# Keys times query into PSUM: the scores of a one-token attention kernel, 16 keys at a time

## The chip, the cores and the metric

The kernel runs on one core of a Trainium2 chip. Such a core has TensorE (PE, matrix products into PSUM), VectorE (DVE), ScalarE (ACT), GpSimd (POOL) and SyncE (SP), which here issues nearly all transfers from the chip's main memory. Each engine has its own list of instructions and waits for others by semaphores. SBUF is the core's working memory of 128 partitions; PSUM is a smaller one of eight banks, each of 512 float32 values per partition. The metric is the time of one execution on the device in microseconds.

## The reference

One decoding step with batch `B` = 2: layer norm, an attention with 32 heads of 128 over a cache of 8192 keys and values per head, and a gate from a small two-layer network.

```python
xn = layernorm(x)                                    # x: 2 x 1 x 512
q = (xn @ wq) as 2 x 32 heads x 1 x 128
scores = einsum("bhqd,bhkd->bhqk", q, k_cache) * 128 ** -0.5     # 8192 keys
p = softmax(scores)
o = einsum("bhqk,bhkd->bhqd", p, v_cache)
s = o as 2 x 1 x 4096 @ wo
g = silu(gelu(layernorm(xn) @ w1 + b1) @ w2 + b2)
out = x + s * g
```

All is float32. K and V are 268 MB each and are read once; that is most of the 559 MB that the kernel reads.

## The kernel before

**Tiling.** The 64 combinations of batch and head are taken two at a time: 32 "pairs" (`N`), numbered 0 to 31. In a pair each of the two heads has 64 partitions, and each partition holds 128 (`KP`) keys of 128 values: a K or V tile of 128 x 16384 float32, 8.4 MB. SBUF has three such buffers: `big0` and `big1` (`KBUF[0]`, `KBUF[1]`) take the K of even and odd pairs, `big2` (`VB`) takes V. Before the pairs begin, a setup computes the query and spreads it so that `Q[:, n, :]` holds in each partition the query of that partition's head, and computes the gate `z`; its weights and intermediate values use the same three buffers and PSUM banks.

**The scores of a pair** are VectorE's work, `scores` (L328). It waits for the K tile, multiplies it by the query and writes the product over K itself (one `tensor_tensor` over 128 x 16384, L332, the query repeated for every key), waits for that, and sums each key's 128 products into `SC` (one `tensor_reduce`, L335). It waits again and takes the maximum over the partition's keys, `MX` (L337). TensorE transposes `MX` into `pm`, VectorE takes from it the negated maximum of each head, `nm` (L339), TensorE spreads that over the partitions (`pn`), and ScalarE computes the exponentials into `PZ` and their sums into `RS` (L351 on). The waits are instructions of their own, made by `take` (L45), which waits for a semaphore and counts it down; by the profile such a wait is one on the engine's own sequencer, "DVEq L45".

**Weighting.** TensorE multiplies `PZ` with V in 32 products (`weighted`, L475); ScalarE copies the sum to `o4`, TensorE folds that into `pt`, and ScalarE keeps it in `OT`. In the time in which TensorE would wait, `unread` (L459) lets it compute products into bank 6 that nobody reads.

**Loops and queues.** VectorE's loop (L342) runs over pairs 0 to 29, two to a turn; the last two pairs stand behind it, the last with K in two halves. ScalarE, TensorE and SP have loops of their own over the same pairs. SP's list (L305 to L325) sets the order of the transfers, all in one queue: K of pair n + 2 when the softmax of pair n has begun (`p_k`, sent by TensorE behind `nm`), then V of pair n + 1 when the weighting of pair n has let go of its buffer (`p_free`). V of the last pair goes to K's buffer, and behind it comes `wo` in eight pieces, into V's buffer.

**The end.** From the kept sums VectorE computes `ZL`, `Z` and `on` (the attention's output, L370 to L377), TensorE multiplies `on` with `wo` as its pieces arrive, 28 columns into `pw` and the rest into `acc` (L526 on), and two VectorE instructions apply the gate and add x.

A single helper line, L51, issues every operation, so the profile's groups are told apart by tile names: `big` is K or V (or the weights that share their place), `sc` the scores.

Of the kernel before, what the change touches and what calls it, by code (L numbers as in the profile page):

```python
# [5 lines left out]
ALU = mybir.AluOpType  # L6
AX = mybir.AxisListType
# [6 lines left out]
class Program:  # L14
# [24 lines left out]
    def wait(self, eng, *tokens):  # L39
        for name, v in self.need(eng, tokens):  # L40
            self.engines[eng].wait_ge(self.sem(name), v)

    def take(self, eng, name, v=1):

        self.engines[eng].wait_ge(self.sem(name), v).then_inc(self.sem(name), -v)  # L45

    def op(self, eng, method, *args, waits=(), sig=None, by=1, quiet=False, **kwargs):
        need = self.need(eng, waits)
        for name, v in need[:-1]:
            self.engines[eng].wait_ge(self.sem(name), v)  # L50
        ins = getattr(self.engines[eng], method)(*args, **kwargs)  # L51
        for name, v in need[-1:]:
            ins._wait_ge(self.sem(name), v)
        if quiet:
            return None
        name = sig or "own_" + eng
        by = 16 if method == "dma_start" else by
        ins.then_inc(self.sem(name), by)
        self.counts[name] += by
        return name, self.counts[name]  # L60


def decode_kernel(nc, x, kc, vc, wq, wo, w1, b1, w2, b2, out):
    P = 128
    B, H, S, DH = kc.shape
# [3 lines left out]
    U = 2  # L69
    HP = P // U  # L70
    KP = S // HP
    HH = H // U
    N = B * HH
# [22 lines left out]
    op, wait, take = pr.op, pr.wait, pr.take  # L96

    def sb(shape, name):
        return nc.alloc_sbuf_tensor(name, list(shape), F32).ap()

    def ps(shape, name):
        return nc.alloc_psum_tensor(name, list(shape), F32).ap()
# [6 lines left out]
    KBUF, VB = rows[:2], rows[2]  # L109
# [24 lines left out]
    Q = sb([P, N, DH], "Q")  # L134
    ident = sb([P, P], "ident")
# [13 lines left out]
    z = sb([P, P], "z")  # L149
# [6 lines left out]
    SC = [sb([P, KP], f"sc{i}") for i in range(2)]  # L156
# [10 lines left out]
    on = sb([P, MB, OC], "on")  # L167
    mod_b = sb([P, R], "mod_b")

    bank = [ps([P, 512], f"bank{i}") for i in range(8)]  # L170
    po = bank[0]
    pm = bank[1]
    pn = bank[2]
    pt = bank[3]
    acc = bank[4][:, :P]
    OA = bank[5][:, :B * (OC + 1)].rearrange("p (b c) -> p b c", c=OC + 1)
# [9 lines left out]
    QH = len(PB) // 2  # L186
# [6 lines left out]
    def pe_n(name, n):  # L193
        return name, n + 1

    t = {}
# [30 lines left out]
    for k in (7, 6, 1, 2, 4, 0):  # L227
# [13 lines left out]
                  op=ALU.add)  # L241
    t["sel"] = op("DVE", "tensor_copy",
                  sel[:, HP:].rearrange("p (b j r) -> p b j r", b=B, r=HG)[:, :, :QT, 0], by_row[:, :B, :],
                  waits=[t["sel0"]])
# [23 lines left out]
    c = op("DVE", "tensor_mul", gu, gh, gh, waits=[a])  # L268
    c = op("DVE", "tensor_scalar", gu, gu, GELU_A, 1.0, op0=ALU.mult, op1=ALU.add, waits=[c])
    c = op("DVE", "tensor_mul", gu, gu, gh, waits=[c])  # L270
    c = op("ACT", "activation", gu, gu, AF.Tanh, scale=GELU_C, waits=[c])
    c = op("DVE", "scalar_tensor_tensor", gu, gu, 1.0, gh, op0=ALU.add, op1=ALU.mult, waits=[c])
# [8 lines left out]
    for part, n0, n1 in (("first", 0, NPB), ("rest", NPB, N)):  # L281
        shape = [BH, n1 - n0, DH]
        t[f"QN {part}"] = op("DVE", "tensor_tensor", out=QN[:, n0:n1, :], in0=q_all.unsqueeze(1).to_broadcast(shape),
                           in1=mine[:, n0:n1].unsqueeze(2).to_broadcast(shape), op=ALU.mult,
                           waits=[t["qall"], t["mine"]])
# [13 lines left out]
    for b in range(B):  # L299
        t["x4"] = op("SP", "dma_start", x4[HB * b::R, :], x[b, 0].rearrange("(j n) -> j n", n=P), sig="d_x4",  # L300
                     waits=[t["x4m"]])
# [26 lines left out]
    def scores(u, q, sems, cuts):  # L328
        k = KBUF[u]
        for name, (c0, c1) in zip(sems, zip(cuts, cuts[1:])):  # L330
            take("DVE", name, 16)
            op("DVE", "tensor_tensor", out=k[:, c0:c1], in0=k[:, c0:c1],  # L332
               in1=q.unsqueeze(1).to_broadcast([P, c1 - c0, DH]), op=ALU.mult, sig="v_t")
            take("DVE", "v_t")
            op("DVE", "tensor_reduce", out=SC[u][:, c0:c1], in_=k[:, c0:c1], axis=AX.X, op=ALU.add, sig="v_r")  # L335
        take("DVE", "v_r", len(sems))
        op("DVE", "tensor_reduce", out=MX, in_=SC[u], axis=AX.X, op=ALU.max, sig="v_mx")  # L337
        take("DVE", "p_m")
        op("DVE", "tensor_reduce", out=nm, in_=pm[:1, :P].rearrange("o (s r) -> o s r", s=U), axis=AX.X,  # L339
           op=ALU.max, negate=True, sig="v_nm")  # L340

    with nc.vector.Fori(0, N // U - 1) as i:  # L342
        take("DVE", "s_q")
        for u in range(U):
            scores(u, Q.rearrange("p (i u) d -> p i u d", u=U)[:, i, u, :], [f"d_k{u}"], (0, KP))
    take("DVE", "s_q")
    scores(0, Q[:, N - U, :], ["d_k0"], (0, KP))
    scores(1, Q[:, N - 1, :], ["d_k1", "d_kl"], HALVES)


    with nc.scalar.Fori(0, N // U) as i:  # L351
        for u in range(U):
# [4 lines left out]
            for s in range(U):  # L357
# [10 lines left out]
                   waits=[t["th"], t["pool"]])  # L368
    shape = [P, N, U * PH]
    t["ZL"] = op("DVE", "tensor_tensor", out=ZL, in0=half.unsqueeze(1).to_broadcast(shape),  # L370
                 in1=RS.unsqueeze(2).to_broadcast(shape), op=ALU.mult, waits=[pe_n("p_z", 0), t["half"]])
# [3 lines left out]
                in1=OT.unsqueeze(2).to_broadcast(shape), op=ALU.mult, waits=[t["OT"], t["blk"]])  # L375
    t["on"] = op("DVE", "tensor_tensor", out=on[:, ::HB, :], in0=OA[:, :, :OC], in1=rl.unsqueeze(2).to_broadcast([P, B, OC]),
                 op=ALU.mult, waits=[t["rl"], t["on0"], pe_n("p_oa", 0)])  # L377
    t["wide"] = op("ACT", "copy", o4, pw, waits=[pe_n("p_w", 0)])
    a = op("DVE", "scalar_tensor_tensor", res, acc, 0.5, gate, op0=ALU.mult, op1=ALU.mult,
           waits=[pe_n("p_acc", 0), t["gate"]])  # L380
    t["res"] = op("DVE", "tensor_add", res, res, x4, waits=[a, t["x4"]])
    t["out"] = op("SP", "dma_start", out.rearrange("b s (j n) -> j (b s) n", n=P), res[::HB, :], sig="d_out",
                  waits=[t["res"]])
# [6 lines left out]
    def mm(dst, w, v, start=True, stop=True, sig=None, waits=(), skip=False):  # L390
        kw = {"skip_group_check": True} if skip else {}
        if sig in PE_EVENTS:
            done.append(sig)
            sig = "pe_setup"
        return op("PE", "matmul", dst, w, v, start=start, stop=stop, waits=waits, sig=sig, quiet=sig is None, **kw)
# [15 lines left out]
    for c in range(ND):  # L411
# [4 lines left out]
        j, k = NF % QT, NF // QT  # L416
# [6 lines left out]
    j, k = NF % QT, NF // QT  # L423
    mm(ph[R * j:R * j + B, k * P:k * P + FT], ones[:1, :B], b1_sb[:, NF * P:], start=False, stop=True, sig="ph")
    by_tile = ident.rearrange("p (j r) -> p j r", r=R)
    for k in range(NH):
        n = min(QT, NF + 1 - k * QT)
        mm(phT[:, k * QT * B:(k * QT + n) * B].rearrange("p (j b) -> p j b", b=B), h_nat[:, k * P:(k + 1) * P],
           by_tile[:, :n, :B], waits=[t["h"]], sig="phT" if k == NH - 1 else None)
    for n in range(NG // QT):  # L430
        for c in range(ND):
            for j in range(QT):
                g = n * QT + j
# [3 lines left out]
    for n in range(NG // QT):  # L437
        for hh in range(HG):
# [3 lines left out]
               waits=[t["sel"], t["qnat"]], sig="pqa" if last else None)  # L442

    for g in range(N // NPB):
        mm(PB[g % len(PB)], sides, QN[:, g * NPB:(g + 1) * NPB, :].rearrange("h n d -> h (n d)"),
           waits=[t["side"], t["QN rest" if g else "QN first"]] + ([t[f"Q{QH}"]] if g >= len(PB) else []),
           sig=f"pb{g}")
    for f in range(NF + 1):
        j = f % QT
        k = P if f < NF else FT  # L450
        mm(pg[R * j:R * j + B, :], hT[:k, f, :], w2_sb[:k, f, :], start=f < QT, stop=f + QT > NF and j != QT - 1,
           waits=[t["hT"], t["w2"], t["mem6"]])
    mm(pg[R * (QT - 1):R * (QT - 1) + B, :], ones[:1, :B], b2_sb, start=False, stop=True, waits=[t["b2"]], sig="pg")
    for j in range(QT):
        mm(pgate[R * j:R * j + MB, :], mod_b[:, :MB], g_nat[:, j * P:(j + 1) * P], waits=[t["g"], t["mod_b"]],
           sig="pgate" if j == QT - 1 else None)
    assert done == PE_EVENTS, done

    def unread(*heads):  # L459

        for n in heads:
            mm(bank[6][:, :n * DH], ident, Q[:, :n, :].rearrange("p n d -> p (n d)"), waits=[t["g"], t[f"Q{QH}"]])

    def softmax(first=False):
        if not first:
            unread(4, 4)
        take("PE", "v_mx")
        op("PE", "transpose", pm[:1, :P], MX, ident, sig="p_m")
        if not first:
            unread(1)  # L470
        take("PE", "v_nm")
        for s in range(U):
            mm(pn[HP * s:HP * (s + 1), :1], srow, nm[:, s:s + 1], sig="p_n" if s == U - 1 else "p_k")

    def weighted(v, last=False):  # L475
        if last:
            unread(4, 2)
        take("PE", "s_pz")
        if not last:
            take("PE", "d_v", 16)  # L480
        for i in range(NT):
            if last and i * JW == HALVES[1]:
                unread(2)
            if last and i * JW in HALVES:
                nc.tensor.wait_ge(pr.sem(f"d_v31{HALVES.index(i * JW)}"), 16)
            j = i % QT
            mm(po[R * j:R * j + U * JW, :], PZ[:, i].rearrange("p s j -> p (s j)"),
               v[:, i * JW:(i + 1) * JW, :].rearrange("p j d -> p (j d)"), start=i < QT, stop=i + QT >= NT,
               sig="p_v" if i == NT - 1 else "p_z" if last and i == 0 else None)
        if last:  # L490
            for b in range(B):
                m = slice(b * HH, (b + 1) * HH)
                mm(OA[:, b, OC:], ZL[:, m].rearrange("p n r -> p (n r)"), ones[:, :1], waits=[t["ZL"]],
                   sig="p_den" if b == B - 1 else None)
            unread(1)
        take("PE", "s_o4")
        for i in range(JW):
            mm(pt[:, :U], o4[:, i * DH:(i + 1) * DH], mod[:, i:U * JW:JW], start=i == 0, stop=i == JW - 1,
               sig="p_t" if i == JW - 1 else "p_free" if i == 0 else None)
# [21 lines left out]
    for b in range(B):  # L521
        h = slice(b * H, (b + 1) * H)
        mm(OA[:, b, :OC], Z[:, h].rearrange("p h r -> p (h r)"), mod, waits=[t["Z"]],
           sig="p_oa" if b == B - 1 else None)
    unread(1)
    for i, (c0, c1) in enumerate(zip(WO_CUTS, WO_CUTS[1:])):  # L526
        for c in range(c0, c1):
            after = [t["on"], t["mem"], (f"d_wo{i}", 16)]
            if c < WIDE:
                j = c % QT  # L530
                mm(pw[R * j:R * j + MB, :], on[:, :, c], wo_sb[:, c, :], start=c < QT, stop=c + QT >= WIDE,
                   waits=after, sig="p_w" if c == WIDE - 1 else None)
# [7 lines left out]
        if c1 == OC - 2:  # L540
            for j in range(QT):
                mm(acc[R * j:R * j + MB, :], mod[:, :MB], o4[:, j * P:(j + 1) * P], start=False, stop=False,
                   waits=[t["wide"]])
# [26 lines left out]
```

## Time and profile before

| | |
|---|---|
| median of the runs | 1300.54 us (2 runs, 1299.89 to 1301.18) |
| the profiled execution | 1299.61 us, span of its profile 1298.3 us |
| VectorE busy | 1135.7 us, 87% of the span, 171 instructions |
| TensorE busy | 460.9 us, 35% |
| ScalarE busy | 72.0 us, 6% |
| DMA | 559.39 MB, mean 431 GB/s, 99.7% of the 16 engines' time in SP's queue |

In the profile's rows the engine is followed by the line, the operation, what it writes and reads, shapes as partitions x elements, and a count. A group's row gives busy time and the mean of one in ns, then the idle time ahead of its instructions and what ended it. In the timeline a row begins with its start and its length in us. TensorE takes a float32 product in two passes, so each product is two rows there. The table of stretches gives for each engine its busy time and, as (x..), its instructions, in the order PE, PEld (weight loads), VectorE, ScalarE, GpSimd; then the TensorE clock granted, the mean busy share of the DMA engines and what they moved.

### The profile page before, as it was taken

To read this page: it belongs to the slowest core of one execution; us is meant where nothing else is said; L and a number is where in the kernel's file an instruction comes from. 1 tells how busy PE (TensorE), PEld (TensorE's weight loads), DVE (VectorE), ACT (ScalarE), POOL (GpSimd) and SP (SyncE) were. 2 spreads that over 40 slices of the span, in tenths; PEclk is the share of its full clock that TensorE was granted. 3 is DMA by queue.
4 is the path that set the end of the run, shared out by engine and by line. 5 is a ranking of instruction groups with operands and counts; after the bars stand their busy time and mean duration, and the time that the engine had idled before them with its cause. 6 is when DMAs were issued, how large, how long until landed. Compare 5 with 4: busy or idle time off the path is not lost. (4 is left out here: it accounts for less than half of the span.)

```text
span 1298.3 us, 7389 instructions
## 1 busy us (share of the span) xinstructions
PE 460.9 (35%) x2958; PEld 148.7 (11%) x2958; DVE 1135.7 (87%) x171; ACT 72.0 (6%) x245; POOL 2.1 (0%) x14
## 2 busy tenths in 40 slices
PE   3813433322433322343322334322334321343337
PEld 1201111001111000111100111100111100111103
DVE  2599999988889988889988888988888988888991
ACT  1100000000000000000000000000000000000000
POOL 0000000000000000000000000000000000000000
PEclk8756776567677556777656777656776666677659
DMA  9999999999999999999999999999999999999998
GB/s 410 436 428 442 430 432 432 428 444 428 438 430 428 440 428 444 428 434 430 428 444 428 440 430 426 440 428 444 428 434 430 430 442 428 440 430 430 423 436 361
DMA packets 11242, 559.39 MB, mean 431 GB/s; under 512 B 1264, under 2 KB 1536, under 8 KB 1892
## 3 DMA queue, kind: packets, MB, share of 16 engines
q1 hardware_dynamic: 11228, 559.30, 99.7%
q8 instruction: 4, 0.07, 0.0%
q10 hardware_dynamic: 8, 0.01, 0.0%
q14 instruction: 2, 0.02, 0.0%
HBM read 559.30 MB, written 0.00 MB: 431 GB/s over the span
## 5 line engine op out<-in xcount | busy, mean ns | idle before, releaser
L51 DVE TENSOR_TENSOR big<-big,Q 128x16384 f32<-128x16384 f32 (+1 forms) x33 | 551.3, 16707 | 73.2 <-DVEq L45 73.2
L51 DVE TENSOR_REDUCE sc<-big 128x128 f32<-128x16384 f32 (+1 forms) x33 | 551.2, 16703 | 4.8
L51 PE MATMUL bank<-big,PZ 128*8 128x512 f32 x2048 | 291.1, 732 | 628.9 <-PEq L45 628.9
L51 PEld LDWEIGHTS bank<-big,PZ 128*8 128x8 f32 x2048 | 60.1, 103 | 832.6 <-issue 832.6
L51 PE MATMUL bank<-Q,ident 128*128 128x512 f32 (+2 forms) x198 | 78.5, 506 | 0.2 <-issue 0.2
L51 ACT COPY o<-bank 128x512 f32<-128x512 f32 x33 | 19.4, 586 | 891.6 <-ACTq L45 880.0
L51 PE MATMUL bank<-ident,MX 128*1 128x128 f32 x32 | 9.3, 291 | 137.9 <-PEq L45 137.8
L51 PE MATMUL bank<-mod,o 128*128 128x2 f32 x256 | 32.8, 250 | 27.4 <-PEq L45 27.4
L51 PEld LDWEIGHTS bank<-mod,o 128*128 128x128 f32 x256 | 31.0, 191 | 55.4 <-issue 55.4
L51 PEld LDWEIGHTS bank<-Q,ident 128*128 128x128 f32 x198 | 33.6, 198 | 16.5 <-issue 16.5
L51 ACT ACTIVATE PZ<-sc,bias 64x128 f32<-64x128 f32 x64 | 25.5, 399 | 6.6 <-ACTq L45 6.2
L51 DVE TENSOR_REDUCE nm<-bank 1x2 f32<-1x128 f32 x32 | 8.9, 279 | 18.9 <-DVEq L45 18.9
L51 DVE TENSOR_TENSOR big<-big,mine 64x512 f32<-64x512 f32 (+1 forms) x2 | 4.5, 2279 | 21.6 <-ACT big L51 21.6
L51 PEld LDWEIGHTS bank<-ident,MX 128*1 128x1 f32 x32 | 2.5, 79 | 162.9 <-issue 162.9
L51 ACT COPY bias<-bank 128x1 f32<-128x1 f32 x32 | 5.1, 159 | 225.2 <-ACTq L45 225.2
L51 PE MATMUL bank<-nm,srow 1*64 1x1 f32 x128 | 10.4, 219 | 10.0 <-PEq L45 9.4
L51 PE MATMUL bank<-big,sides 64*128 64x512 f32 x16 | 12.6, 958 | 3.7 <-DVE big L51 3.7
L51 DVE TENSOR_REDUCE MX<-sc 128x1 f32<-128x128 f32 x32 | 9.2, 286 | 4.7
L51 PE MATMUL bank<-big,xnT 128*2 128x512 f32 x64 | 9.3, 748 | 10.3 <-DMA big<-in_A_wq_dram 10.3
L51 ACT ACTIVATION_READ_ACCUMULATOR PZ<-sc,bias x64 | 11.8, 184 | 0.0
L51 DVE SCALAR_TENSOR_TENSOR res<-bank,gate 128x128 f32<-128x128 f32 x1 | 0.3, 292 | 12.1 <-PE bank L51 12.1
L51 PEld LDWEIGHTS bank<-nm,srow 1*64 1x64 f32 x128 | 8.6, 165 | 16.2 <-issue 16.2
(78 smaller groups left out, 74.8 us busy)
## 6 DMA issues: line engine op xcount, KB each, us to landing
big<-in_A_k_cache_dram SPq DMA_DIRECT2D x2, 4096.0 KB, 35.9
big<-in_A_v_cache_dram SPq DMA_DIRECT2D x2, 4096.0 KB, 35.9
big<-in_B_w_dram SPq DMA_DIRECT2D x1, 2752.0 KB, 10.2
big<-in_B_w_dram SPq DMA_DIRECT2D x1, 2560.0 KB, 52.1
big<-in_A_wo_dram SPq DMA_DIRECT2D x1, 2560.0 KB, 14.7
big<-in_A_wo_dram SPq DMA_DIRECT2D x1, 2048.0 KB, 19.3
big<-in_A_wo_dram SPq DMA_DIRECT2D x1, 1536.0 KB, 22.5
big<-in_A_wo_dram SPq DMA_DIRECT2D x1, 1024.0 KB, 24.5
```

Of the source, the lines that this page charges most:

```text
L51: ins = getattr(self.engines[eng], method)(*args, **kwargs)
```

## The change

VectorE's products of pairs 2 to 29 no longer go back to the K tile. Banks 4 to 7 become one PSUM tensor `wide` of 2048 float32 per partition, which holds the products of 16 keys (`STEP`). A pair's scores come from eight steps: a product of 16 keys with the query, written to `wide`, and a sum from `wide` into 16 columns of `SC`. There is one `wide`, so each product waits for the sum before it, and each sum for its product, by `take`. Pairs 0 and 1 stand ahead of VectorE's loop and pairs 30 and 31 behind it, with the old code; ahead of the loop VectorE also waits for `z`, the last value that the setup reads from banks 4 to 7. `pn` moves from bank 2 to the second half of bank 1, and the products that nobody reads go to bank 2 in place of bank 6. What SP issues and waits for is unchanged.

```diff
+    wide = ps([P, 4 * 512], "wide")
+    bank = [ps([P, 512], f"bank{i}") for i in range(4)] + [wide[:, i * 512:(i + 1) * 512] for i in range(4)]
+    STEP = 4 * 512 // DH
+    prod = wide.rearrange("p (j d) -> p j d", d=DH)
...
-    pn = bank[2]
+    pn = bank[1][:, 2 * P:]
...
-        take("DVE", "v_r", len(sems))
+        maxima(u, len(sems))
+
+    def products(u, q):
+        take("DVE", f"d_k{u}", 16)
+        for c in range(0, KP, STEP):
+            if c:
+                take("DVE", "v_r")
+            op("DVE", "tensor_tensor", out=prod, in0=KBUF[u][:, c:c + STEP],
+               in1=q.unsqueeze(1).to_broadcast([P, STEP, DH]), op=ALU.mult, sig="v_t")
+            take("DVE", "v_t")
+            op("DVE", "tensor_reduce", out=SC[u][:, c:c + STEP], in_=prod, axis=AX.X, op=ALU.add, sig="v_r")
+        maxima(u, 1)
+
+    def maxima(u, n):
+        take("DVE", "v_r", n)
         op("DVE", "tensor_reduce", out=MX, in_=SC[u], axis=AX.X, op=ALU.max, sig="v_mx")
...
-    with nc.vector.Fori(0, N // U - 1) as i:
+    take("DVE", "s_q")
+    for u in range(U):
+        scores(u, Q[:, u, :], [f"d_k{u}"], (0, KP))
+    wait("DVE", t["z"])
+    with nc.vector.Fori(0, N // U - 2) as i:
         take("DVE", "s_q")
         for u in range(U):
-            scores(u, Q.rearrange("p (i u) d -> p i u d", u=U)[:, i, u, :], [f"d_k{u}"], (0, KP))
+            products(u, Q.rearrange("p (i u) d -> p i u d", u=U)[:, i + 1, u, :])
...
-            mm(bank[6][:, :n * DH], ident, Q[:, :n, :].rearrange("p n d -> p (n d)"), waits=[t["g"], t[f"Q{QH}"]])
+            mm(bank[2][:, :n * DH], ident, Q[:, :n, :].rearrange("p n d -> p (n d)"), waits=[t["g"], t[f"Q{QH}"]])
```

VectorE's list at the start of its loop, where an even pair begins (`d_k0` is the arrival of its K, `v_t` a product done, `v_r` a sum done; the row `ISA` takes the loop's register for the address in `Q`). Before:

```order
L342 UNCONDITIONAL_BRANCH
L51 ISA [waits s_q,d_k0]
L51 TENSOR_TENSOR big0<-big0,Q 128x16384
L51 TENSOR_REDUCE sc0<-big0 128x128 [waits v_t]
L51 TENSOR_REDUCE MX<-sc0 128x1 [waits v_r]
```

The same place now:

```order
L363 UNCONDITIONAL_BRANCH [waits own_ACT]
L51 ISA [waits s_q,d_k0]
L51 TENSOR_TENSOR wide<-big0,Q 128x2048
L51 TENSOR_REDUCE sc0<-wide 128x16 [waits v_t]
L51 TENSOR_TENSOR wide<-big0,Q 128x2048 [waits v_r]
```

The one product of 16384 elements has become the first of eight of 2048, the second of which waits for the first sum; `own_ACT` at the branch is the wait for `z`.

VectorE's list in the middle of the loop, where the even pair ends with `MX` and `nm` and the odd pair begins (`p_m` is TensorE's transpose of `MX`). Before:

```order
L51 TENSOR_REDUCE sc0<-big0 128x128 [waits v_t]
L51 TENSOR_REDUCE MX<-sc0 128x1 [waits v_r]
L51 TENSOR_REDUCE nm<-bank1 1x2 [waits p_m]
L51 ISA [waits d_k1]
L51 TENSOR_TENSOR big1<-big1,Q 128x16384
```

Now:

```order
L51 TENSOR_TENSOR wide<-big0,Q 128x2048 [waits v_r]
L51 TENSOR_REDUCE sc0<-wide 128x16 [waits v_t]
L51 TENSOR_REDUCE MX<-sc0 128x1 [waits v_r]
L51 TENSOR_REDUCE nm<-bank1 1x2 [waits p_m]
L51 ISA [waits d_k1]
L51 TENSOR_TENSOR wide<-big1,Q 128x2048
```

The end of a pair and the step to the next stand as before; in front of them are now eight sums and eight products in place of one each.

More of the change, by code (lines that the diff above doesn't have):

```diff
@@ L168, in decode_kernel @@
     mod_b = sb([P, R], "mod_b")
-    bank = [ps([P, 512], f"bank{i}") for i in range(8)]
+    wide = ps([P, 4 * 512], "wide")
+    bank = [ps([P, 512], f"bank{i}") for i in range(4)] + [wide[:, i * 512:(i + 1) * 512] for i in range(4)]
+    STEP = 4 * 512 // DH
+    prod = wide.rearrange("p (j d) -> p j d", d=DH)
     po = bank[0]
     pm = bank[1]
-    pn = bank[2]
+    pn = bank[1][:, 2 * P:]
     pt = bank[3]
```

## The prediction

> **What bounds the kernel now.** I read the chain of waits first, then the DMA rates, then VectorE's timeline in the steady part. The chain (start us, us, what):
>
> ```profile
> by line: DMA big<-in_A_wo_dram 2.0%; PE bank L51 0.1%; SPq L51 0.1%; DVE res L51 0.0%; issue 0.0%; DVEq L50 0.0%
> ...
> 1268.70 25.32 DMA big<-in_A_wo_dram
> ...
> 1294.06 1.73 PE bank L51 x40
> ```
>
> The end is set by the last transfer, wo. It sits in one queue behind all K and V loads, so the next question is whether that queue ever rests. One row of the table by stretches covers pairs 6 to 29 (DMA share and GB/s stand last), and the timeline of VectorE and of SP's issues shows one period of it (start us, us, engine, instruction, in brackets the idle time before it):
>
> ```profile
> 269.37:1198.13 928.76, 307.55 (x1992) 97.55 (x1992) 840.26 (x96) 45.27 (x168) 0.00 (x0) 0.67 1.00 434
> ```
>
> ```profile
> 518.95 17.22 DVE L51 TENSOR_REDUCE sc<-big 128x128 f32<-128x16384 f32 x1
> ...
> 520.83 8.39 PE L51 MATMUL bank<-big,PZ 128*8 128x512 f32 x64 [21.67 <-PEq L45]
> ...
> 530.62 0.33 SPq L51 DMA_DIRECT2D big<-in_A_v_cache_dram  x1
> 536.31 0.29 DVE L51 TENSOR_REDUCE MX<-sc 128x1 f32<-128x128 f32 x1
> 537.17 0.28 DVE L51 TENSOR_REDUCE nm<-bank 1x2 f32<-1x128 f32 x1 [0.57 <-DVEq L45]
> 538.19 0.33 SPq L51 DMA_DIRECT2D big<-in_A_k_cache_dram  x1
> 540.27 17.23 DVE L51 TENSOR_TENSOR big<-big,Q 128x16384 f32<-128x16384 f32 x1 [2.83 <-DVEq L45]
> 578.97 17.23 DVE L51 TENSOR_TENSOR big<-big,Q 128x16384 f32<-128x16384 f32 x1 [2.83 <-DVEq L45]
> ```
>
> DMA share is 1.00 over the stretch, and 928.76 / 24 = 38.70 us per pair is the time of a K and a V tile (38.70 x 434 GB/s = 16.8 MB). VectorE waits 2.83 us in front of each product, named after its own queue because the wait is a separate instruction. That it waits for K is seen from the load issued at 538.19:
>
> ```profile
> big<-in_A_k_cache_dram SPq DMA_DIRECT2D x31, 40.6
> big<-in_A_v_cache_dram SPq DMA_DIRECT2D x31, 28.1
> ```
>
> 538.19 + 40.6 = 578.8, and the product that reads it starts at 578.97. So DMA sets the pace, and VectorE has 38.70 - 2.83, about 35.9 us, of its own work per pair. How long VectorE takes when K is there already, a stretch shortly after the start shows:
>
> ```profile
> 158.43 0.28 DVE L51 TENSOR_REDUCE nm<-bank 1x2 f32<-1x128 f32 x1 [0.67 <-DVEq L45]
> 158.67 17.23 DVE L51 TENSOR_TENSOR big<-big,Q 128x16384 f32<-128x16384 f32 x1
> ...
> 195.03 17.22 DVE L51 TENSOR_TENSOR big<-big,Q 128x16384 f32<-128x16384 f32 x1 [0.39 <-DVEq L45]
> ```
>
> One pair is 36.36 us with the loop's jump at its end. In the middle of the loop's body the product starts 0.04 us before `nm` is over; across the jump it starts 0.39 us after. VectorE's cover in a pair is thus under 3 us, and the change spends it on instruction count.
>
> **The change, VectorE.** Per pair it replaces one product and one sum over 16384 elements by eight of each over 2048. The elements are the same; what grows is what each instruction costs beside its elements. The groups by shape (busy us, mean ns, idle before):
>
> ```profile
> L51 DVE TENSOR_TENSOR big<-big,Q 128x16384 f32<-128x16384 f32 x31 | 534.0, 17225 | 73.2 <-DVEq L45 73.2
> L51 DVE TENSOR_REDUCE sc<-big 128x128 f32<-128x16384 f32 x31 | 533.8, 17220 | 4.5
> L51 DVE TENSOR_REDUCE sc<-big 128x64 f32<-128x8192 f32 x2 | 17.4, 8686 | 0.3
> L51 DVE TENSOR_TENSOR big<-big,Q 128x8192 f32<-128x8192 f32 x2 | 17.4, 8676 | 0.0
> L51 DVE TENSOR_REDUCE MX<-sc 128x1 f32<-128x128 f32 x32 | 9.2, 286 | 4.7
> L51 DVE TENSOR_REDUCE nm<-bank 1x2 f32<-1x128 f32 x32 | 8.9, 279 | 18.9 <-DVEq L45 18.9
> ```
>
> - Product: (17225 - 8676) / 8192 = 1.0436 ns an element, and 127 ns fixed. At 2048 elements: 2264 ns.
> - Sum: (17220 - 8686) / 8192 = 1.0417 ns an element, and 152 ns fixed. At 2048: 2286 ns. (At 128 elements this gives 285 ns; `MX`, a reduction of that length, has 286.)
> - Eight of both: 8 x 4.550 = 36.40 us, against 34.45 us now: +1.95 us.
> - Gaps. Each product and each sum but the first now waits for the one before by a separate wait instruction. The sums wait so today, 4.5 / 31 = 0.145 us each, `MX` 4.7 / 32 = 0.147 us. There is one such gap inside a pair now and there will be 15: 15 x 0.146 = 2.19 us.
> - The rest of a pair stays: gap 0.147, `MX` 0.286, wait for TensorE's transpose 18.9 / 32 = 0.59, `nm` 0.279, and the step to the next pair, -0.04 and +0.39 by turns, mean 0.18. Sum 1.48 us.
>
> P = 36.40 + 2.19 + 1.48 = 40.07 us per pair. The same sum for the pair of today gives 34.45 + 0.145 + 1.48 = 36.07, where the timeline has 36.36 with the jump and some 0.4 less without, mean 36.15: it agrees to 0.1 us.
>
> 40.07 is more than the 38.70 of DMA: VectorE becomes the bound by 1.37 us a pair, and its 2.83 us of waiting are gone.
>
> Three costs no row shows at this place:
>
> - *Writing products to PSUM.* VectorE's only PSUM writes in the trace are memsets, which give no price beside an SBUF one. From below, its fixed part could vanish whole, -127 ns a product: 8 x 28 x 0.127 = -28.4 us. From above I use the dearest PSUM read of the next point. I take 0, the value that reads show.
> - *Reading them from PSUM.* `nm` reads 128 elements from PSUM in 279 ns, `MX` 128 from SBUF in 286. Three rows of 128 elements more, and two short copies:
>
> ```profile
> L51 DVE SCALAR_TENSOR_TENSOR res<-bank,gate 128x128 f32<-128x128 f32 x1 | 0.3, 292 | 12.1 <-PE bank L51 12.1
> L51 DVE TENSOR_TENSOR res<-res,x 128x128 f32<-128x128 f32 x1 | 0.3, 292 | 0.1
> ...
> L51 DVE SCALAR_TENSOR_TENSOR gate<-th,z 128x128 f32<-128x128 f32 x1 | 0.3, 268 | 0.0
> ...
> L51 DVE COPY xnT<-bank 128x8 f32<-128x8 f32 x1 | 0.2, 167 | 1.6 <-PE bank L51 1.6
> ...
> L51 DVE COPY big<-ident 128x8 f32<-128x8 f32 x1 | 0.2, 166 | 0.0
> ```
>
>   The extra for a PSUM source lies between -7 ns (`nm`) and +24 ns (292 against 268); a plain SBUF sum has the same 292, and the copies differ by 1. I take 0; the ends are -1.6 and +5.4 us over 8 x 28 sums. [...]
> - *A product whose `Q` address comes from the loop's register, right behind a wait.* Today such a product follows `nm` by 158.67 - 158.43 = 0.24 us, its register step included. The last pair's, with a fixed address, follows it by 0.21:
>
> ```profile
> 1233.72 0.28 DVE L51 TENSOR_REDUCE nm<-bank 1x2 f32<-1x128 f32 x1 [0.57 <-DVEq L45]
> 1233.93 8.67 DVE L51 TENSOR_TENSOR big<-big,Q 128x8192 f32<-128x8192 f32 x1
> ```
>
>   So 0 to 0.03 us each, over 7 x 28 products 0 to +5.9 us. I take 0.
>
> **The other edits** cost nothing that I can find. The new wait for `z` in front of pair 2: ScalarE has written `z` by 66.3 us, pair 2 starts at 122.73.
>
> ```profile
> 66.00 0.27 ACT L51 COPY z<-bank 128x128 f32<-128x128 f32 x1 [0.53 <-PE bank L51]
> ...
> 122.73 17.22 DVE L51 TENSOR_TENSOR big<-big,Q 128x16384 f32<-128x16384 f32 x1 [0.42 <-DVEq L45]
> ```
>
> `pn` in another bank and TensorE's filler products in bank 2 are as many and as long as before. K is still released only by `p_k`, after `nm`, so leaving K unchanged frees no buffer sooner. SP's order is untouched, but what it waits for comes later. After `nm` of a pair ends (537.45) the next K but one is issued within 1 us (538.19); the weighting with V takes 8.39 us, and its V buffer is free about 1.5 us behind that (520.83 + 8.39 = 529.22, V issued at 530.62). So with VectorE as the bound V is issued some 12 us after `nm`, while K is still under way, and the queue does not run dry between them. Both have landed 1 + 38.70 us after `nm`, and the next pair but one needs that K at 40.07. A V that lands a little late only moves the weighting, which TensorE must finish before the next transpose, some 40 us on. What is late next behind the DMA's pace is thus VectorE alone.
>
> **The end.** Pairs 30 and 31 keep the old code and wait for no K today:
>
> ```profile
> 1198.13 17.23 DVE L51 TENSOR_TENSOR big<-big,Q 128x16384 f32<-128x16384 f32 x1 [2.74 <-DVEq L45]
> ...
> 1269.01 0.29 DVE L51 TENSOR_REDUCE MX<-sc 128x1 f32<-128x128 f32 x1
> ...
> 1272.28 3.62 PE L51 MATMUL bank<-big,PZ 128*8 128x512 f32 x32
> ...
> 1283.88 4.64 PE L51 MATMUL bank<-big,on 128*17 128x512 f32 x36
> ```
>
> Pair 30 starts at 122.73 + 28 x 40.07 = 1244.7 instead of 1198.13: +46.6 us, and all up to the first product with wo at 1283.88 moves by that. Behind it, today, wo's pieces arrive one by one until 1294.02. Were they all there, 28 products of two rows each at 3.62 / 32 = 0.113 us take 6.3 us, and the last 40 rows 1.73: end at about 1292.0 instead of 1295.8. This slack of 3.8 us is won back: when VectorE is late, DMA is ahead. V of pair 31 is issued at about 1282 and done by 1302, wo 20 us later at 1322, and the first product with wo comes at 1330. So +46.6 - 3.8 = +42.8 us. The profiled execution took 1299.61 us (span 1298.3): 1342.4. The median of the runs is 0.93 us above it: 1343 us.
>
> **The rivals.** What a measurement here can tell from no change I take as 2%, 26 us.
>
> - *Forecast, chance 0.72*: 1343 us; with the bounds above, from 1342.4 - 28.4 + 0.9 = 1315 to 1342.4 + 5.4 + 5.4 + 5.9 + 0.9 = 1360.
> - *PSUM dearer than any read shows, 0.13.* If both the write and the read pay the 24 ns that one pair of rows allows, 16 x 28 x 0.024 = 10.8 us: 1354 us. Slower as well. Against it: the four other rows show none of it. [...]
> - *The gaps shrink, 0.13; not slower.* The place is the 15 gaps of a pair. A wait that stands on the instruction itself costs 0.04 us in this trace (5.73 + 0.67 = 6.40, next start 6.44):
>
> ```profile
> 5.73 0.67 DVE L51 BATCH_NORM_STATS2 st_xn<-big 2x6 f32<-2x512 f32 x1
> 6.44 0.17 DVE L51 BATCH_NORM_AGGREGATE mv_xn<-st_xn 2x2 f32<-2x6 f32 x1
> ```
>
>   If behind short instructions or PSUM writes the separate wait took no longer than that, P = 40.07 - 15 x 0.106 = 38.48. Pair 30 would start 2.1 us later than now, inside the slack of 3.8: no change, 1300 us. It decides at P = 39.47 (gaps of 0.106 us) for within 2%, and at 38.54 (0.044 us) for no change. Against it: all 31 gaps behind products and 32 in front of `MX` are 0.145 to 0.147 us with the same instruction. [...]
> - *DMA speeds up because VectorE no longer writes to SBUF, 0.02; faster.* It needs VectorE out of the way too. DMA moves 438 GB/s while VectorE writes a product and 439 while it only reads:
>
> ```profile
> 501.60:518.80 17.20, 0.00 (x0) 0.00 (x0) 17.20 (x1) 0.00 (x0) 0.00 (x0) 0.50 1.01 438
> 519.00:536.00 17.00, 11.24 (x76) 3.36 (x76) 17.00 (x1) 0.75 (x2) 0.00 (x0) 0.87 1.02 439
> ```
>
>   One part in 400 of 38.70 us is 0.09 us a pair: 1297 us. Over 2% faster would need 1.0 us a pair.
>
> **How the numbers follow.** The likeliest case gives 1343 us. Its bounds, 1315 to 1360, hold the second case's 1354 as well; left out are no change, the faster case and the far ends, together under 2 in 10. Slower: 0.72 + 0.13, less a little for a write so cheap that the time ends below 1326, and as much back for gaps that shrink only in part: 0.85. Same 0.13, faster 0.02.
>
> **What will show it.** Products and sums of 128x2048 at 2.26 and 2.29 us; gaps of 0.146 us between them; a pair of 40.1 us; no wait of 2.8 us ahead of a pair's first product; DMA share under 1.00 (38.70 / 40.07 = 0.97) in the stretch of pairs 6 to 29; `on` at about 1330 us and no wait for wo behind it. Wrong would be: VectorE still waiting for K, a product into PSUM that lasts clearly other than 2.26 us, or gaps other than 0.146.

## The result and the profile after

The changed kernel takes 1361.44 us (median of two runs, 1360.73 to 1362.15) against 1300.54: slower by 4.7%, ratio 1.0471 with a 95% interval of 1.0454 to 1.0488. The forecast was 1343 us, slower, with a range up to 1360: the way was right, the size was too small and the time lies just above the range. The profiled execution took 1362.15 us, 62.5 us more than that of before.

The groups of VectorE by shape (busy us, mean ns of one, idle before them), after:

```profile
L51 DVE TENSOR_TENSOR wide<-big,Q 128x2048 f32<-128x2048 f32 x224 | 515.1, 2299 | 37.5 <-DVEq L45 10.8
L51 DVE TENSOR_REDUCE sc<-wide 128x16 f32<-128x2048 f32 x224 | 513.4, 2292 | 32.7
...
L51 DVE TENSOR_REDUCE nm<-bank 1x2 f32<-1x128 f32 x32 | 8.9, 279 | 21.5 <-DVEq L45 21.5
```

The stretch that was DMA's before, pairs 6 to 29, now has a DMA share of 0.97 and 414 GB/s in place of 1.00 and 434:

```profile
269.37:1198.13 928.76, 302.77 (x1909) 99.16 (x1909) 852.49 (x412) 43.38 (x161) 0.00 (x0) 0.66 0.97 414
```

VectorE's timeline, first around a jump of its loop, then in the middle of the body (start us, us, instruction, in brackets the idle time):

```profile
203.34 0.28 DVE L51 TENSOR_REDUCE nm<-bank 1x2 f32<-1x128 f32 x1 [0.67 <-DVEq L45]
204.19 2.30 DVE L51 TENSOR_TENSOR wide<-big,Q 128x2048 f32<-128x2048 f32 x1 [0.57 <-DVEq L45]
206.63 2.29 DVE L51 TENSOR_REDUCE sc<-wide 128x16 f32<-128x2048 f32 x1
209.21 2.30 DVE L51 TENSOR_TENSOR wide<-big,Q 128x2048 f32<-128x2048 f32 x1 [0.28 <-DVEq L45]
...
406.77 0.28 DVE L51 TENSOR_REDUCE nm<-bank 1x2 f32<-1x128 f32 x1 [0.67 <-DVEq L45]
407.02 2.30 DVE L51 TENSOR_TENSOR wide<-big,Q 128x2048 f32<-128x2048 f32 x1
409.46 2.29 DVE L51 TENSOR_REDUCE sc<-wide 128x16 f32<-128x2048 f32 x1
411.90 2.30 DVE L51 TENSOR_TENSOR wide<-big,Q 128x2048 f32<-128x2048 f32 x1
```

The 2.8 us of waiting for K ahead of a pair are gone; what stands there is 0.6 us at most. Between products and sums lie gaps of 0.15 us (409.46 + 2.29 = 411.75, next start 411.90). From `nm` to `nm` a pair takes 40.27 us in the middle of the body and about 40.92 behind a jump. The start of pair 2 and of pair 30, and the end:

```profile
122.62 2.30 DVE L51 TENSOR_TENSOR wide<-big,Q 128x2048 f32<-128x2048 f32 x1 [0.26 <-DVEq L45]
...
1259.37 17.23 DVE L51 TENSOR_TENSOR big<-big,Q 128x16384 f32<-128x16384 f32 x1
...
1330.35 0.28 DVE L51 TENSOR_REDUCE MX<-sc 128x1 f32<-128x128 f32 x1
...
1335.10 5.25 PE L51 MATMUL bank<-big,PZ 128*8 128x512 f32 x32
...
1348.33 7.93 PE L51 MATMUL bank<-big,on 128*17 128x512 f32 x56
```

(1259.37 - 122.62) / 28 = 40.60 us a pair: VectorE sets the pace. The chain of waits no longer begins with a transfer. It runs through TensorE's products with wo, which find all of wo there:

```profile
1348.33 7.96 PE bank L51 x56
1356.29 0.02 issue
1356.31 0.59 ACT o L51
1356.90 0.04 issue
1356.95 0.90 PE wide L51 x24
```

So the forecast's mechanism is what one sees, and 19.7 us are missing from its sum (62.5 - 42.8). The rows place them. A pair is 40.60 us and not 40.07: 28 x 0.53 = 14.8 us. From pair 30's start to the first product with wo it is 88.96 us (1348.33 - 1259.37) where before had 85.75: 3.2 us. And from there to TensorE's end it is about 9.5 us and not the 8.1 that I allowed: 1.4 us. Most of the rest lies outside the span, which is 62.0 us longer.

### The profile page after: what moved, and what is told of

Its sections match the earlier page's. It is cut to its first block, busy times and chain, and to the rows that moved or that the text cites. A ratio compares the mean times of both kernels' runs of the same rounds, so it can differ in the third digit from the quotient of the medians.

```text
span 1360.3 us, 8168 instructions
## 1 busy us (share of the span) xinstructions
PE 471.1 (35%) x2958; PEld 157.4 (12%) x2958; DVE 1199.2 (88%) x563; ACT 72.0 (5%) x245; POOL 2.1 (0%) x14
## 5 line engine op out<-in xcount | busy, mean ns | idle before, releaser
L51 DVE TENSOR_TENSOR wide<-big,Q 128x2048 f32<-128x2048 f32 x224 | 515.1, 2299 | 37.5 <-DVEq L45 10.8
L51 DVE TENSOR_REDUCE sc<-wide 128x16 f32<-128x2048 f32 x224 | 513.4, 2292 | 32.7
L51 PE MATMUL bank<-Q,ident 128*128 128x512 f32 (+2 forms) x198 | 85.8, 549 | 0.1
L51 DVE TENSOR_TENSOR big<-big,Q 128x16384 f32<-128x16384 f32 (+1 forms) x5 | 69.0, 13801 | 2.9 <-DVEq L45 2.7
L51 DVE TENSOR_REDUCE sc<-big 128x128 f32<-128x16384 f32 (+1 forms) x5 | 69.0, 13806 | 0.7
L51 PEld LDWEIGHTS bank<-Q,ident 128*128 128x128 f32 x198 | 39.2, 232 | 16.9 <-issue 16.9
## 6 DMA issues: line engine op xcount, KB each, us to landing
big<-in_A_wo_dram SPq DMA_DIRECT2D x1, 2560.0 KB, 15.7
```

## The experiments

Ten kernels, each compared with the kernel before on the same chip. Two theories stood against each other. **Mine**: eight times as many instructions, with a wait between each two, put VectorE above DMA's pace; PSUM as such costs next to nothing. **The rival**: writing to and reading from PSUM costs the time.

### The same steps without PSUM

```diff
-            op("DVE", "tensor_tensor", out=prod, in0=KBUF[u][:, c:c + STEP],
+            op("DVE", "tensor_tensor", out=KBUF[u][:, c:c + STEP], in0=KBUF[u][:, c:c + STEP],
...
-            op("DVE", "tensor_reduce", out=SC[u][:, c:c + STEP], in_=prod, axis=AX.X, op=ALU.add, sig="v_r")
+            op("DVE", "tensor_reduce", out=SC[u][:, c:c + STEP], in_=KBUF[u][:, c:c + STEP], axis=AX.X, op=ALU.add,
+               sig="v_r")
```

> The eight steps of a pair as in the changed kernel, with the same waits, but each product is written back over its 16 keys of K in SBUF and summed from there: the step size alone, without PSUM. Theory (writing to PSUM makes the product dearer: 2299 ns in the changed kernel, 2264 by the slope of the SBUF products before; the sum 2292 against 2286): products of 2264 ns, sums of 2286, a pair shorter by 8 x 0.041 = 0.33 us, 28 pairs by 9 us: about 1353 us. Rival (a product of 2048 elements lasts 2299 ns anywhere, PSUM has no part in it): 2299 ns, 1361 us. If the 0.56 us in front of the second product of each turn of the loop is the loop's own (a jump), it stays; if it is PSUM's, it goes.

Measured: 1358.47 us (1357.59 to 1358.99), ratio 1.0449 (1.0432 to 1.0467). VectorE's groups:

```profile
L51 DVE TENSOR_TENSOR big<-big,Q 128x2048 f32<-128x2048 f32 x224 | 513.4, 2292 | 37.7 <-DVEq L45 10.8
L51 DVE TENSOR_REDUCE sc<-big 128x16 f32<-128x2048 f32 x224 | 512.1, 2286 | 32.6
```

Between the two, and nearer the rival: a product of 2048 elements in SBUF lasts 2292 ns, so 28 of the 35 ns that my slope had missed have nothing to do with PSUM. PSUM itself adds 7 ns to the write and 6 to the read, 28 x 8 x 0.013 = 2.9 us, which is the difference in time (1361.44 - 1358.47). The gap ahead of the second product behind a jump (0.55 us in the loop's first turn, about 0.27 in the others) stays, so it isn't PSUM's either. Nearly the whole loss, 58 of 61 us, comes with the step size and its waits alone.

### The waits on the instructions themselves

```diff
-            if c:
-                take("DVE", "v_r")
...
+            if n:
+                a._wait_ge(pr.sem("v_r"), n)
+            a.then_inc(pr.sem("v_r"), 1)
...
+            a._wait_ge(pr.sem("v_r"), n + 1)
+            a.then_inc(pr.sem("v_r"), 1)
+            n += 2
```

> As the changed kernel, with products in PSUM, but the 15 waits inside a pair stand on the products and sums themselves, which wait for rising counts of one semaphore; one separate wait takes all 16 counts back ahead of MX. Theory (the separate wait instruction makes most of the 0.146 us gap; a wait on the instruction costs 0.04 us, as between the two layer norm statistics): a pair shorter by 15 x 0.106 = 1.6 us, 40.6 - 1.6 = 39.0 us, still above the 38.7 us of DMA, so 28 x 1.6 = 45 us less: about 1317 us. Rival (the gap is the time in which a finished instruction's signal reaches the next one, whoever carries the wait): 0.146 us again, 1361 us.

Measured: 1311.81 us (1308.99 to 1313.01), ratio 1.0094 (1.0077 to 1.0111). The timeline in the middle of the body:

```profile
627.41 2.30 DVE L51 TENSOR_TENSOR wide<-big,Q 128x2048 f32<-128x2048 f32 x1
629.74 2.29 DVE L51 TENSOR_REDUCE sc<-wide 128x16 f32<-128x2048 f32 x1
632.07 2.30 DVE L51 TENSOR_TENSOR wide<-big,Q 128x2048 f32<-128x2048 f32 x1
```

The gaps are 0.03 to 0.04 us (627.41 + 2.30 = 629.71, then 629.74). The products still go to PSUM, still last 2300 ns, and each still waits for its sum; only the form of the wait is another (the separate instruction waits and counts the semaphore down, here the product or sum waits itself), and 49.6 of the 61 us are gone. That is 5 us more than I expected; the additional time ahead of the second product behind a jump went as well (0.03 to 0.04 us there too, in all 14 turns). A pair is 38.85 us.

### As many steps, no exposed wait

```diff
+        times(0)
+        for c in range(0, KP, STEP):
+            if c + STEP < KP:
+                times(c + STEP)
+            take("DVE", f"v_t{c // STEP % 2}")
+            op("DVE", "tensor_reduce", out=SC[u][:, c:c + STEP], in_=KBUF[u][:, c:c + STEP], axis=AX.X, op=ALU.add,
+               sig="v_r")
```

`times(c)` issues the product of the step that begins at key c, over K itself, with the semaphores `v_t0` and `v_t1` by turns.

> Eight steps in SBUF, in place over K as in the run before the last, but each product is issued one step ahead of the sum of the step before it, so that a sum waits for a product that ended one instruction earlier and no product waits for a sum. As many instructions, no exposed wait. Theory (the gaps decide, as a pair's 15 x 0.146 us): a pair of 36.4 + 1.5 - 0.6 = 37.3 us on VectorE, less than DMA's 38.7, VectorE waits for K again, about 1301 us. Rival (the number of instructions decides, the waits are hidden behind the end of each instruction anyway): the same time as with the steps in SBUF and exposed waits, 1353 us.

Measured: 1300.03 us (1299.70 to 1300.50), ratio 0.9998 (0.9989 to 1.0008). The pair's start and its first steps:

```profile
616.02 0.28 DVE L51 TENSOR_REDUCE nm<-bank 1x2 f32<-1x128 f32 x1 [0.57 <-DVEq L45]
618.47 4.49 DVE L51 TENSOR_TENSOR big<-big,Q 128x2048 f32<-128x2048 f32 x2 [2.17 <-DVEq L45]
622.88 2.28 DVE L51 TENSOR_REDUCE sc<-big 128x16 f32<-128x2048 f32 x1
625.08 2.28 DVE L51 TENSOR_TENSOR big<-big,Q 128x2048 f32<-128x2048 f32 x1
```

Each step begins 0.08 us before the one ahead of it has ended (622.88 + 2.28 = 625.16, then 625.08), and VectorE waits 2.17 us for K again. There are sixteen products and sums a pair as in the run with the steps in SBUF, and 58 us less. The eight waits of the sums are left, and are met before they are reached; the seven of the products are gone. The steps still have a price, which DMA hides: in pairs 3 to 6, where K is there already, a pair takes 36.60 us in the middle of the body and 37.04 to 37.20 behind a jump, against 35.9 and 36.4 in the kernel before and 40.17 and 40.9 in the run with exposed waits. With products in PSUM this order was not run.

### Half of the change

```diff
+        h = KP // 2
+        op("DVE", "tensor_tensor", out=KBUF[u][:, :h], in0=KBUF[u][:, :h],
+           in1=q.unsqueeze(1).to_broadcast([P, h, DH]), op=ALU.mult, sig="v_t")
+        take("DVE", "v_t")
+        op("DVE", "tensor_reduce", out=SC[u][:, :h], in_=KBUF[u][:, :h], axis=AX.X, op=ALU.add, sig="v_r")
+        op("DVE", "tensor_reduce", out=SC[u][:, :h], in_=KBUF[u][:, :h], ...
-        for c in range(0, KP, STEP):
+        for c in range(h, KP, STEP):
```

> The first 64 keys of a partition as one product and one sum in SBUF as in the kernel before, the other 64 in four steps through PSUM as in the changed kernel: half of the change. Theory (the longer of VectorE and DMA sets a pair's time): 8.68 + 8.69 + 4 x (2.30 + 2.29) + 9 x 0.146 + 1.55 + 0.2 for the loop = 38.8 us on VectorE against DMA's 38.7: the cost is nearly all hidden, 1300 to 1306 us. Rival (PSUM products cost the kernel in proportion to how many there are, by whatever way): half of the 61 us, 1331 us.

Measured: 1309.05 us (1308.35 to 1309.77), ratio 1.0068 (1.0052 to 1.0085): far from half the loss, but above what I had expected. A pair takes 38.74 us, as worked out (38.8). The bound that I set it against was wrong: the pairs 2 to 29 of before take (1198.13 - 122.73) / 28 = 38.41 us on average, because VectorE starts late and catches up in the first of them, so the point from which VectorE decides is near 38.54, as the prediction has it, and not 38.70. That makes 28 x 0.2 = 5.6 us; most of the rest is the end, where TensorE takes 17.1 us from the last `MX` to the first product with wo and not 14.9. The half of the keys in one piece gives a row that matters below; two of its 30 products are the last pair's, and the 28 of the loop have a mean of 8692 ns:

```profile
L51 DVE TENSOR_TENSOR big<-big,Q 128x8192 f32<-128x8192 f32 x30 | 260.7, 8691 | 6.8 <-DVEq L45 6.8
```

### Half as many jumps

Four pairs in a turn of VectorE's loop instead of two:

```diff
-    with nc.vector.Fori(0, N // U - 2) as i:
+    with nc.vector.Fori(0, (N - 2 * U) // (2 * U)) as i:
+        for m in range(2 * U):
```

> The changed kernel with four pairs in each turn of VectorE's loop in place of two: 7 jumps instead of 14, all else alike. In the changed kernel the pair behind a jump takes 40.92 us from nm to nm and the other 40.27: 0.49 us instead of -0.03 ahead of its first product, and 0.27 instead of 0.15 ahead of its second. Theory (both belong to the jump): 7 x 0.65 = 4.5 us less, about 1357 us. Rival (it is the start of an even pair, wherever it stands): 1361 us.

Measured: 1358.94 us (1358.57 to 1359.29), ratio 1.0453 (1.0436 to 1.0471): 2.5 us less, between the two. The loop's branch on VectorE (seven, with their durations in ns and the start of the first and the last in us), then the pair behind the first of them, and the third pair of the turn that begins there, an even one with no jump ahead of it:

```profile
L363 DVEq COMPARE_BRANCH  x7: 50/56/67, 284.5 to 1256.3; - x7
...
284.40 0.28 DVE L51 TENSOR_REDUCE nm<-bank 1x2 f32<-1x128 f32 x1 [0.67 <-DVEq L45]
285.25 2.30 DVE L51 TENSOR_TENSOR wide<-big,Q 128x2048 f32<-128x2048 f32 x1 [0.57 <-DVEq L45]
287.70 2.29 DVE L51 TENSOR_REDUCE sc<-wide 128x16 f32<-128x2048 f32 x1
290.26 2.30 DVE L51 TENSOR_TENSOR wide<-big,Q 128x2048 f32<-128x2048 f32 x1 [0.27 <-DVEq L45]
...
365.67 0.28 DVE L51 TENSOR_REDUCE nm<-bank 1x2 f32<-1x128 f32 x1 [0.67 <-DVEq L45]
366.02 2.30 DVE L51 TENSOR_TENSOR wide<-big,Q 128x2048 f32<-128x2048 f32 x1
```

Behind each jump back the first product still starts 0.50 to 0.57 us after `nm`, and the second 0.26 to 0.27 us after its sum. The third pair starts 0.07 us after `nm`, not 0.5. So the two delays belong to the jump, as the theory has it, and the rival is wrong. The gain is smaller than 4.5 us because smaller delays appear at places without a jump: the third pair's 0.07 in place of -0.03, and in the middle of the fourth pair a product that starts 0.28 us after its sum in place of 0.15, together some 1.8 us over seven turns. What these last two are the runs don't tell.

### TensorE kept busy

```diff
-            unread(4, 4)
+            unread(*[4] * 32)
         take("PE", "v_mx")
```

> The changed kernel with 32 products that nobody reads instead of 2 ahead of each transpose of MX, so that TensorE idles a few us there and not 17 to 20. Theory (TensorE, idle before it is asked, runs at a lower clock: 0.67 us until nm in place of 0.57, and 3.2 us more between the last MX and the attention's output): 28 to 30 pairs by 0.1 us and 3 us in the end, together 6 us less: about 1356 us. Rival (the wait for the transpose and the slower end have another cause, or the filler takes the clock down elsewhere): 1361 us or more.

Measured: 1390.73 us (1388.06 to 1391.51), ratio 1.0693. The dose was wrong:

```profile
637.67 27.71 PE L51 MATMUL bank<-Q,ident 128*128 128x512 f32 x64
```

The filler takes 27.7 us of each pair, and with TensorE's other work that is more than a pair of VectorE's: VectorE waited 12.2 us for pair 1's transpose, up to 1.36 in the loop and 5.5 and 5.4 in the last two pairs. So the time of this run does not answer the question. The same holds for the three edits together with that filler:

> The changed kernel, products in PSUM by 16 keys as it has them, with the three edits together: waits on the products and sums themselves, four pairs in a turn, 32 products of filler. Theory (these waits, jumps and TensorE's clock are what puts VectorE above DMA): a pair of 38.58 - 0.10 + 0.13 = 38.6 us, just under DMA's 38.70, VectorE waits for K again now and then: 1300 to 1304 us. Rival (PSUM products keep a cost of their own that the rows of VectorE do not show): as with the waits on the instructions alone, 1312 us, less the 6 us of the filler and the 4 us of the jumps only where those are real.

Measured: 1390.30 us (1387.65 to 1391.55), the same as with the filler alone, since TensorE set the pace in both. With a smaller dose:

> The changed kernel with 18 products of filler ahead of each transpose of MX in place of 2. With 32 they took 27.7 us, 0.87 us each, and TensorE's own work came to more than a pair's time; 18 take 15.6 us of the 19.3 us that TensorE has in the end, and more elsewhere. Theory (TensorE's low clock after idling costs 0.1 us a pair in the wait for the transpose and 3 us in the end): 0.57 us until nm, products with V in 3.62 us and not 5.25 for the first half of the last weighting, 6 us less: about 1356 us. Rival (these have another cause): 1361 us.

Measured: 1358.77 us (1358.07 to 1360.58), ratio 1.0456 (1.0438 to 1.0473): 2.7 us less, half of what was expected. The end went as the theory has it. TensorE idles 3.5 us ahead of the last transpose and not 17.4, `nm` waits 0.57 us, and the products behind it are faster:

```profile
1331.08 0.27 PE L51 MATMUL bank<-ident,MX 128*1 128x128 f32 x1 [3.48 <-PEq L45]
...
1335.29 3.79 PE L51 MATMUL bank<-big,PZ 128*8 128x512 f32 x32
...
1347.06 6.23 PE L51 MATMUL bank<-big,on 128*17 128x512 f32 x56
```

3.79 us against 5.25 for the first half of the weighting, 6.23 against 7.93 for wo. In the loop the wait for `nm` stayed at 0.67: there TensorE idled some 24 us before, and the filler, 15.7 us long, still leaves it idle for 10 to 12 us.

### The three edits together, products in PSUM

> As the run with the three edits together (waits on the products and sums themselves, four pairs in a turn, filler), but 18 products of filler in place of 32. Theory (waits, jumps and TensorE's clock are what puts VectorE above DMA): a pair of 38.6 us, DMA's 38.70 sets the pace again, 1300 to 1304 us. Rival (products in PSUM keep a cost that VectorE's rows do not show): 1309 us or more, what the waits on the instructions alone gave less the jumps.

Measured: 1309.70 us (1309.42 to 1310.02), ratio 1.0075 (1.0058 to 1.0092). Above the theory's range, and what the rival gives, so the time alone does not tell them apart. The trace shows `nm` waiting 0.57 us in 23 of the loop's 28 pairs, and a pair of 38.73 us on average (the next expectation has 38.65); in pairs 30 and 31 V comes late, the weighting and so the filler begin late, and `MX` is ready first:

```profile
1283.71 0.27 PE L51 MATMUL bank<-ident,MX 128*1 128x128 f32 x1
1283.82 0.39 PE L51 MATMUL bank<-Q,ident 128*128 128x128 f32 x2
1284.13 0.28 DVE L51 TENSOR_REDUCE nm<-bank 1x2 f32<-1x128 f32 x1 [4.29 <-DVEq L45]
```

> The three edits together as in the run before, with 13 products of filler in place of 18. There the pairs of the loop took 38.65 us, DMA's pace, but in the last two pairs, where the weighting starts late because V comes late, the filler still ran when MX was ready: 2.33 and 4.29 us until nm in place of 0.57, 5.5 us in all. Theory (nothing but that is left): 13 products are 4.4 us shorter, 4 to 5 us come back: 1304 to 1306 us. Rival (products in PSUM keep a cost that VectorE's rows do not show): 1309 us again.

Measured: 1306.57 us (1304.57 to 1308.44), ratio 1.0052 (1.0035 to 1.0069), the profiled execution 1304.90. The median is just above the theory's range: 3.1 us came back and not 4 to 5. The 4.29 us became 1.53. A pair takes 38.70 us, still a little over the 38.54 from which VectorE decides, which makes 4.5 us; the filler's rest in the last pair makes 1.0. The span of the profiled execution is 5.1 us longer than before, so in this trace nothing of size stays for a cost of PSUM that VectorE's rows don't show. Two of the four executions took 1308.2 and 1308.4, and what they lost the trace of a faster one can't tell. None of the versions is faster than the kernel before, which has DMA as its bound throughout.

## Why the prediction was off

The mechanism of the pairs was right, and terms of its sum were too small; the end has a mechanism that the prediction left out, a slower TensorE (granted clock 0.78 behind the last transpose, where before had 1.00). The largest error is the product's length, read off a line through two rows of different kinds: 6.3 us. With that term alone put right the forecast would have been 1349 us and its range would have ended at 1366. The end (4.6 us), the steps at the jumps (3 us), PSUM (2.9 us) and TensorE's wait (2.2 us) make up most of the rest.

**What bounds it: right.** DMA's share fell to 0.97 as forecast, the waits of 2.83 us for K went, and the products with wo wait for no transfer at the end.

**Gaps: right.** The forecast's 0.146 us is what stands there (32.7 / 224 = 0.146 ahead of the sums), 15 times a pair. The rival by which they shrink was wrong for this kernel, but its premise was right: a wait on the instruction costs 0.035 us also behind these instructions, and that run is within 1% of before. For these products and sums the runs show three cases: separate waits that are met late cost 0.146 us, waits on the instruction 0.035, and waits met early leave a start 0.08 us before the end of the instruction ahead.

**PSUM: near the 0 that was taken, and the bounds held.** 7 ns a write (2299 against 2292) and 6 a read (2292 against 2286), where -127 to +24 and -7 to +24 were allowed.

**The product's length: wrong, 28 x 8 x 0.028 = 6.3 us.** The step that failed is the line through two rows, 17225 ns at 16384 elements and 8676 at 8192. The second row came from the last pair alone, whose products have a fixed address and start 0.07 to 0.08 us before the instruction ahead has ended. The half tile in the loop lasts 8692 (the run with half of the change), which gives 1.0416 ns an element, nearly the sum's own slope, and 159 ns fixed: 2292 at 2048, where SBUF has 2292. The last pair's row is thus 16 ns too short to stand for the loop's. The traces tell which of its two differences goes with that. In the changed kernel pairs 1 and 30 have the same old code and a fixed address; the product of pair 1 begins 0.07 us before `nm` ends, that of pair 30 (1259.37, above) 0.14 us after:

```profile
86.20 0.28 DVE L51 TENSOR_REDUCE nm<-bank 1x2 f32<-1x128 f32 x1 [0.67 <-DVEq L45]
86.41 17.20 DVE L51 TENSOR_TENSOR big<-big,Q 128x16384 f32<-128x16384 f32 x1
```

They last 17202 and 17225 ns, and in each of the ten runs 17201 to 17203 and 17225 to 17227. A fixed address alone doesn't shorten the row, then; the early start goes with it. The last pair's two products begin early, behind `nm` (8670 ns) and behind a sum (8682). An error of 16 ns in a row of 8.7 us became 28 ns in one of 2.3 us, and it counted 224 times.

**TensorE's wait and the places in the loop: each too small.** I took the mean of all pairs, 0.59 us, for the wait on the transpose; in the changed kernel, where TensorE idles 13 to 26 us ahead of the transposes, it is 0.67 in every pair, 28 x 0.08 = 2.2 us. The trace of before had shown it: in its first five pairs, where TensorE idles 5.7 to 19.6 us ahead of the transpose, the wait is 0.67, as in the row at 158.43 of the prediction. The step between pairs was given 0.39 us at a jump, and is about 0.50, with 0.12 more ahead of the second product; both belong to the jump, by the run with half as many. Halved over the pairs, that is 0.11 us a pair, 3 us. With PSUM's 2.9 us and the product's 6.3, this is the 14.8 us of the pairs to 0.4.

**The end: wrong, 4.6 us.** "All up to the first product with wo moves by that" and 0.113 us a row for wo took TensorE's speed at the end of before, where weighting and filler had kept it at work until 1269.3 and its clock stood at 1.00. The edit that I cost at nothing, the filler "as many and as long as before", no longer covers the wait: with VectorE as the bound TensorE idles 17.4 us ahead of the last transpose. The granted clock (the figure ahead of the DMA share) in that wait, behind it, and in the products with wo, after:

```profile
1313.50:1330.70 17.20, 0.00 (x0) 0.00 (x0) 16.84 (x3) 0.00 (x0) 0.00 (x0) 0.63 1.00 419
1331.00:1348.00 17.00, 16.39 (x99) 6.41 (x98) 1.54 (x6) 1.89 (x7) 0.00 (x0) 0.78 0.51 211
1348.30:1358.00 9.70, 9.22 (x96) 3.97 (x96) 0.13 (x1) 0.58 (x1) 0.00 (x0) 0.82 0.00 0
```

And before, from the last transpose on:

```profile
1269.40:1284.00 14.60, 13.54 (x103) 5.92 (x107) 1.72 (x6) 1.89 (x7) 0.00 (x0) 1.00 0.97 415
```

The run with 18 products of filler brought back 1.5 us of the weighting and 1.7 us of wo, which is the greater part of it. Its clock in the products with wo stood at 1.00, and 28 of them took 6.23 us, close to the prediction's 6.3.

**The range** held bounds for what no row showed and none for the terms that I read off rows. Of the 19 us named here PSUM's 2.9 fall under the first and all else under the second, and all have one sign.

## What to carry to other kernels

Before cutting one long instruction into eight, count the waits that come between them and see whether they are met early: here sixteen instructions a pair cost 58 us where each waits for the one just ahead by a separate instruction, 12 us with the wait on the instruction (PSUM's part included), and nothing that shows with the sums one step behind, where the 0.7 us a pair that they still cost lies under DMA's time. A fixed cost that is multiplied by hundreds must be read from rows of one kind, started alike, since here a slope through two long rows of different kinds hid 28 ns of 2292. And when an engine stops being the one that is waited for, ask what the others do in the time that they now idle: here TensorE came back at a granted clock of 0.78 in place of 1.00.

## What was not expected of the hardware

Products that start 0.07 to 0.08 us before the instruction ahead has ended have shorter rows. In the run with no exposed wait the products of 2048 elements last 2283 ns on average, where the one behind the wait for K at 618.47 has 2293; the last pair's two of 8192 have 8670 and 8682 against 8692 in the loop. How early the start is seems to matter: the products of before that start 0.04 us ahead of `nm`'s end last 17225 to 17226, like those behind a wait. And in the loop's code there are places at which VectorE starts 0.1 to 0.5 us late although nothing that it waits for is missing: the larger ones, 0.5 us and 0.12 us, stand behind the loop's jump whether its body has two pairs or four, two smaller ones came with the longer body. Both are seen, neither is explained here.
